# Rows of 768 bytes and products with the identity for k and q of block 0

## The chip, the core and the metric

The kernel runs on one core of a Trainium2 chip. Its engines are TensorE (PE: matmuls, and PEld: the weight loads that go with them), VectorE (DVE), ScalarE (ACT), GpSimd (POOL) and SyncE (SP), which here issues the DMAs. The metric is the device time of one execution in microseconds; smaller is better.

## The reference

The program is an attention layer followed by a feed-forward layer. For each of 4 batches and 8 heads (768 positions, 64 numbers a head):

```python
k_sum = k.reshape(B, H, nb, block, D).max(axis=3)      # 24 blocks of 32 keys
v_sum = v.reshape(B, H, nb, block, D).mean(axis=3)
scores_l = scale * q @ k^T   # only where |row - column| < 16
scores_s = scale * q @ k_sum^T + log(block)
a = softmax(concat(scores_l, scores_s))
attn = a @ concat(v, v_sum)
```

Then `x = attn` as 3072 tokens of 512 numbers, `h = x @ w_in` (512 x 2048), `g = h * cos(h)`, `out = g @ w_out` (2048 x 512). All is float32.

## The kernel before

The 3072 tokens are cut into 8 blocks of 384 (half a batch each). A block's attention is four groups of two heads, named `a`, `b`, `c`, `d`; so `a0` is group a of block 0, `d1` group d of block 1. For a group, k and q have to stand with the 64 numbers of a head on partitions and the positions along the free axis. The two heads lie on partitions 0 to 63 and 64 to 127.

The feed-forward layer runs in steps: a step takes 128 of the 2048 columns of `w_in`, multiplies them with a block's x (lines 726 and 738, 384 columns a matmul), forms the gate on ACT and DVE, and multiplies with 128 rows of `w_out` (line 786, 512 columns a matmul). Weights come in through a slice: DMA (lines 391, 395), two steps on ACT (403, 409), a join and a high part on DVE (416, 372), a low part on DVE or POOL (376).

The order of all work on all engines is written out by hand in one string, `ORDER`. Each token is a unit: `a0.tk.1.5` turns the second half of k of group a0 into bank 5, `a0.cq.v` copies the turned q out on VectorE, `a0.ks.0` takes the block maxima of k, `a0.sc` the scores, `a0.ex` the exponentials, `h7.w.5` is a matmul of the identity with itself that has no use for the result, `w1.lo.p` the low part of weight slice 1 on GpSimd. Every engine works through its instructions in this order; SP issues all DMAs of the start in one queue, and an issue that waits holds up those behind it.

In blocks 0 and 1 (where the first string of `TURNS` is 0) q is loaded as it lies in memory, 128 positions by partition in three chunks, and turned by TensorE, three transposes of 128 x 128 for each group (`turn_q`, line 503). k is loaded once for a batch, with block 0, and covers both halves: six chunks, six transposes (`turn_k`, line 516). From block 2 on VectorE does the turning. A chunk of a head is 64 float32, so a DMA packet of these loads has 256 bytes; one DMA is issued for each head (line 454). There are 16 of them for block 0, and 9216 packets: for each of four groups 2 x 128 x 6 of k and 2 x 128 x 3 of q.

Of the kernel before, what the change touches and what calls it, by code (L numbers as in the profile page):

```python
# [180 lines left out]
def tile_kernel(  # L181
# [11 lines left out]
    nc = tc.nc  # L193

    B, H, S, D = q.shape
    NT, DM = out.shape
    DF = w_in.shape[1]
    P = 128
# [6 lines left out]
    TB = S // 2  # L205
    U = TB // QT
    NG = NPAIR
    QC = TB // P
# [66 lines left out]
    ident = const.tile([P, P], F32, name="ident")  # L275
# [79 lines left out]
    def bank(i):  # L355
        return banks[:, i, :]
# [72 lines left out]
    class Group:  # L429
# [29 lines left out]
        def load_q(self):  # L459
            if self.qn is None:  # L460
                self.qn = att.tile([P, QC, P], F32, name="qn")
            self.load_heads(self.qn, q[self.b, :, self.base : self.base + TB, :], self.squares)

        def load_k(self):
            if self.kn is None:
                self.kn = att.tile([P, KC, P], F32, name="kn")
            self.load_heads(self.kn, k[self.b], self.squares)

        def load_v(self):
            b, h0, base, vn = self.b, 2 * self.pr, self.base, self.vn  # L470
# [28 lines left out]

        def turn_q(self, i):  # L500
            self.qT = bank(i)[:, :TB]
            for c in range(QC):
                nc.tensor.transpose(out=self.qT[:, c * P : (c + 1) * P], in_=self.qn[:, c, :], identity=ident)

# [6 lines left out]
                eng.tensor_scalar_mul(self.qd, self.qT, -SCALE)  # L511

        def turn_k(self, half, i):
            kT = self.kT[half] = bank(i)[:, :TB]
            for c in range(QC):
                nc.tensor.transpose(  # L516
                    out=kT[:, c * P : (c + 1) * P], in_=self.kn[:, half * QC + c, :], identity=ident
                )

        def square_q(self):  # L520
            nc.vector.transpose(out=self.qd, in_=self.qn.rearrange("p c n -> p (c n)"))
# [405 lines left out]
    class Warm:  # L927

        def products(self, i):
# [11 lines left out]
            q="load_q", k="load_k", v="load_v", m="load_vs", tq="turn_q", tk="turn_k", qt="square_q", kt="square_k", pt="square_p", po="move_out", pi="move_in", cq="place_q",  # L941
# [95 lines left out]
```

## Time and profile before

| | |
|---|---|
| median of 3 runs | 633.5 us (633.4 to 634.74) |
| the profiled execution | 633.6 us, of which its span is 631.9 us |
| PE busy | 621.1 us (98%) |
| DVE, ACT, POOL busy | 422.1, 323.9, 204.6 us |
| chain that ended last | PE 92%, DVE 4%, SP's queue 2% |

Times in the rows count from the span's start. A busy share is an average over stages: the first 62 us hold the attention of blocks 0 and 1 beside the first steps of the feed-forward layer, and the other 570 us mostly the feed-forward layer. Matmuls overlap in the array, so the distance between two starts tells more of their price than the duration of one. PE's granted clock is shown as 1.00 in all stretches.

### The profile page before, as it was taken

How to read it: one execution, taken by the hardware profiler on the slowest of the kernel's cores; microseconds unless marked ns; L12 is line 12 of the kernel's file. 1: busy time of each engine (PE TensorE's matmuls, PEld its weight loads, DVE VectorE, ACT ScalarE, POOL GpSimd, SP SyncE). 2: the span in 40 equal slices, each digit the busy share in tenths (PEclk: the TensorE clock that was granted, in tenths of full speed). 3: DMA queues.
4: the chain of work that ended last, by engine and by line, in shares of the span. 5: the costliest groups of instructions: out<-in, count | busy, mean ns of one | idle time of the engine just before them, and what ended most of it. 6: DMA issues, size and time to landing. Idle time of an engine off the chain costs nothing.

```text
span 631.9 us, 12130 instructions
## 1 busy us (share of the span) xinstructions
PE 621.1 (98%) x4568; PEld 544.3 (86%) x4568; DVE 422.1 (67%) x814; ACT 323.9 (51%) x606; POOL 204.6 (32%) x218
## 2 busy tenths in 40 slices
PE   8989999999999999999999999999999999999997
PEld 5667989889889889898988898898898988889895
DVE  4789897896666677577766765656766676544334
ACT  3888886776544454445563634344443463422222
POOL 6593422344503341234452431221431232100101
PEclk9999999999999999999999999999999999999999
DMA  9989939624455447423444544513432431400001
GB/s 223 261 220 272 297 123 250 145 54 123 122 143 133 112 95 174 102 61 108 109 110 126 117 93 102 121 47 77 108 98 61 117 75 56 114 35 17 1 1 50
DMA packets 170058, 73.52 MB, mean 116 GB/s; under 512 B 136848, under 2 KB 158864, under 8 KB 170000
## 3 DMA queue, kind: packets, MB, share of 16 engines
q1 hardware_dynamic: 169856, 72.62, 45.3%
q8 instruction: 36, 0.59, 0.4%
q14 instruction: 22, 0.18, 0.1%
q10 hardware_dynamic: 144, 0.13, 0.1%
HBM read 54.43 MB, written 16.52 MB: 112 GB/s over the span
## 4 chain that ended last, share of the span: by engine, by line
PE 92%; DVE 4%; SPq 2%; DMA 1%; issue 1%; ACT 1%; POOL 0%; POOLq 0%; DVEq 0%
PE banks L786 41%; PE banks L726 40%; PE banks L683 3%; PE banks L567 3%; PE banks L930 1%; SPq L475 1%; DVE stage L416 1%; PE banks L738 1%; PE banks L579 1%; SPq L483 1%; PE banks L516 0%; PE banks L909 0%; DMA late<-in_v_dram 0%; DMA x<-in_v_dram 0%; DVE kd L535 0%
## 5 line engine op out<-in xcount | busy, mean ns | idle before, releaser
L726 PE MATMUL banks<-xh,w 128*128 128x384 f32 x976 | 255.5, 337 | 0.5 <-DVE t L758 0.5
L786 PE MATMUL banks<-w,gh 128*128 128x512 f32 x768 | 196.5, 392 | 0.1
L726 PEld LDWEIGHTS banks<-xh,w 128*128 128x128 f32 x976 | 176.8, 188 | 3.1 <-issue 0.8
L786 PEld LDWEIGHTS banks<-w,gh 128*128 128x128 f32 x768 | 142.6, 188 | 31.4 <-DVE gh L372 1.8
L726 PE MATMUL banks<-xl,w 128*128 128x384 f32 x488 | 163.2, 334 | 0.0
L376 POOL TENSOR_TENSOR gl<-t,gh 128x384 fp32r<-128x384 f32 x63 | 65.9, 1048 | 283.3 <-DVE gh L372 147.8
L746 ACT ACTIVATE t<-banks 128x384 int32<-128x384 f32 x128 | 62.0, 488 | 126.8 <-PE banks L726 59.7
L749 DVE SCALAR_TENSOR_TENSOR t<-t,banks 128x384 f32<-128x384 int32 x128 | 69.1, 546 | 68.3 <-ACT t L746 67.6
L786 PE MATMUL banks<-w,gl 128*128 128x512 f32 x384 | 108.0, 392 | 0.0
L754 ACT ACTIVATE t<-t 128x384 f32<-128x384 f32 x128 | 65.9, 523 | 63.4 <-DVE t L749 63.1
L726 PEld LDWEIGHTS banks<-xl,w 128*128 128x128 f32 x488 | 91.6, 188 | 0.4
L758 DVE TENSOR_TENSOR t<-t,banks 128x384 f32<-128x384 f32 x128 | 69.4, 547 | 33.1 <-ACT t L754 32.1
L786 PEld LDWEIGHTS banks<-w,gl 128*128 128x128 f32 x384 | 71.6, 188 | 15.7 <-POOL gl L376 0.5
L370 ACT CAST gh<-t 128x384 fp32r<-128x384 f32 x66 | 33.5, 511 | 43.5 <-DVE t L758 25.5
L630 POOL TENSOR_TENSOR sc<-sc,r 128x720 f32<-128x720 f32 x28 | 39.0, 1392 | 43.5 <-DVE r L627 41.0
L602 POOL TENSOR_TENSOR sc<-sc,m 128x720 f32<-128x720 f32 x24 | 34.3, 1433 | 49.6 <-DVE m L594 49.6
L376 DVE TENSOR_TENSOR gl<-t,gh 128x384 fp32r<-128x384 f32 x65 | 36.8, 569 | 12.5 <-ACT gh L370 7.5
L372 DVE CAST gh<-t 128x384 fp32r<-128x384 f32 x62 | 23.1, 373 | 18.1 <-PE banks L786 14.9
L586 DVE SCALAR_TENSOR_TENSOR sc<-banks,mask 128x360 f32<-128x360 f32 x48 | 24.5, 523 | 12.5 <-PE banks L567 12.2
L620 DVE TENSOR_REDUCE r<-sc 128x6 f32<-128x726 f32 x24 | 21.6, 902 | 13.8 <-ACT sc L609 13.8
L376 POOL TENSOR_TENSOR w<-stage,w 128x1024 fp32r<-128x1024 f32 x8 | 19.8, 2470 | 31.3 <-DVE w L372 20.0
L609 ACT ACTIVATE sc<-sc 128x720 f32<-128x720 f32 x24 | 19.4, 807 | 19.0 <-POOL sc L602 18.8
(121 smaller groups left out, 621.4 us busy)
## 6 DMA issues: line engine op xcount, KB each, us to landing
pd<-stage SPq DMA_DIRECT2D x24, 384.0 KB
late<-in_moe_w_out_dram SPq DMA_DIRECT2D x16, 511.6 KB
late<-in_moe_w_in_dram SPq DMA_DIRECT2D x16, 510.5 KB
pt<-pd SPq DMA_DIRECT2D x72, 96.0 KB
vn<-in_v_dram SPq DMA_DIRECT2D x50, 120.0 KB
out_dram<-stage SPq DMA_DIRECT2D x23, 256.0 KB
kn<-in_v_dram SPq DMA_DIRECT2D x24, 192.0 KB
kn<-in_k_dram SPq DMA_DIRECT2D x48, 96.0 KB
```

The lines of the kernel that those rows point to most:

```text
L370: eng.copy(out=out, in_=in_)
L372: eng.tensor_copy(out=out, in_=in_)
L376: eng.tensor_tensor(out=lo, in0=src, in1=hi.bitcast(F32), op=ALU.subtract)
L586: nc.vector.scalar_tensor_tensor(out=self.sc.rearrange("p (c h) n -> p c h n", h=2)[:, :, hh, :], in0=self.sp[hh], scalar=SCALE, in1=mask[ ...
L602: nc.gpsimd.tensor_tensor(out=self.sc, in0=self.sc, in1=self.m.unsqueeze(2).broadcast_to([P, U, NK]), op=ALU.subtract)
L630: nc.gpsimd.tensor_tensor(out=self.sc, in0=self.sc, in1=self.r.unsqueeze(2).broadcast_to([P, U, NK]), op=ALU.mult)
L726: nc.tensor.matmul(out=self.h, lhsT=w_of(name, self.f)[:, c * P : (c + 1) * P], rhs=x_of(self.blk, part, c), start=n == 0, stop=n == last,)
L746: nc.scalar.activation(out=self.t.bitcast(I32), in_=self.h, func=AF.Copy, scale=1.0 / TWO_PI, bias=0.25)
L749: nc.vector.scalar_tensor_tensor(out=self.t, in0=self.t.bitcast(I32), scalar=-TWO_PI, in1=self.h, op0=ALU.mult, op1=ALU.add)
L754: nc.scalar.activation(out=self.t, in_=self.t, func=AF.Sin, scale=-1.0, bias=-0.5 * math.pi)
L758: nc.vector.tensor_tensor(out=self.t, in0=self.t, in1=self.h, op=ALU.mult)
L786: nc.tensor.matmul(out=accs[self.run][i], lhsT=g[:, i * P : (i + 1) * P], rhs=w_of(name, self.f), start=self.first and n == 0, stop=self.l ...
```

## The change

For block 0 alone, q and k are loaded with three neighbouring positions in one row: partition p holds positions 3p, 3p+1 and 3p+2 of a head (of k two such halves), 192 float32 or 768 bytes in one packet. That is still one DMA for each head, and 3072 packets for the 16 DMAs. Chunk c of a head then holds every third position. The turn is no longer a transpose of a chunk of both heads: it is one product with the identity for each head and chunk, with the chunk (128 partitions, 64 columns) as weights and the identity (128 columns) as the moving operand. Its 64 x 128 result goes to the partitions of its head, into every third column from c on, so that the positions stand in their order. `turn_q` of block 1 and everything behind the turns are as before; so is `ORDER`.

```diff
         def load_q(self):
             if self.qn is None:
                 self.qn = att.tile([P, QC, P], F32, name="qn")
-            self.load_heads(self.qn, q[self.b, :, self.base : self.base + TB, :], self.squares)
+            src = q[self.b, :, self.base : self.base + TB, :]
+            if self.blk:
+                self.load_heads(self.qn, src, self.squares)
+            else:
+                self.load_rows(self.qn, src)
+
+        def load_rows(self, t, src):
+
+            n = t.shape[1] // QC
+            view = t.rearrange("p c n -> p (c n)").rearrange("p (h m x) -> p h m x", h=2, m=n)
+            for hh in range(2):
+                nc.sync.dma_start(
+                    out=view[:, hh],
+                    in_=src[2 * self.pr + hh].rearrange("(m p c) d -> p m (c d)", p=P, c=QC),
+                )
+
+        def turn_rows(self, to, t, half):
+
+            n = t.shape[1] // QC
+            view = t.rearrange("p c n -> p (c n)").rearrange("p (h m c d) -> p h m c d", h=2, m=n, c=QC)
+            to = to.rearrange("p (n c) -> p n c", c=QC)
+            for c in range(QC):
+                for hh in range(2):
+                    nc.tensor.matmul(
+                        out=to[hh * D : (hh + 1) * D, :, c], lhsT=view[:, hh, half, c], rhs=ident,
+                        start=True, stop=True,
+                    )
...
         def turn_q(self, i):
             self.qT = bank(i)[:, :TB]
+            if not self.blk:
+                self.turn_rows(self.qT, self.qn, 0)
+                return
...
         def turn_k(self, half, i):
-            kT = self.kT[half] = bank(i)[:, :TB]
-            for c in range(QC):
-                nc.tensor.transpose(
-                    out=kT[:, c * P : (c + 1) * P], in_=self.kn[:, half * QC + c, :], identity=ident
-                )
+            self.kT[half] = bank(i)[:, :TB]
+            self.turn_rows(self.kT[half], self.kn, half)
```

`load_k` calls `load_rows` in the same way. On PE the first units of the program stood so before (L930 are the matmuls without use, L516 turns of k, L554 masks, L503 turns of q, L579 scores; `late_105` holds k of group a, `late_107` and `late_106` hold q of b and a):

```order
L930 MATMUL banks<-ident 128x512 x3
L516 MATMUL banks<-ident,late_105 128x128 x6
L554 LDWEIGHTS early
L554 MATMUL banks<-early 128x360
L554 LDWEIGHTS early
L554 MATMUL banks<-early 128x360
L503 MATMUL banks<-ident,late_107 128x128 x3
L503 MATMUL banks<-ident,late_106 128x128 x3
L930 MATMUL banks<-ident 128x512
L579 MATMUL banks<-kd_93,qd 64x96
```

They stand so now, the lines behind the insertion 29 further on, and both kinds of turn on line 485:

```order
L959 MATMUL banks<-ident 128x512 x3
L485 MATMUL banks<-ident,late_105 64x128 x12
L583 LDWEIGHTS early
L583 MATMUL banks<-early 128x360
L583 LDWEIGHTS early
L583 MATMUL banks<-early 128x360
L485 MATMUL banks<-ident,late_107 64x128 x6
L485 MATMUL banks<-ident,late_106 64x128 x6
L959 MATMUL banks<-ident 128x512
L608 MATMUL banks<-kd_93,qd 64x96
```

Nothing has changed its place; each turn of three products has become one of six. The other turns of block 0 on PE, behind the scores of group a, stood so before (`x_2_116` is k of c, `late_105` k of b, `late_108` q of c, `kn` k of d):

```order
L516 MATMUL banks<-ident,x_2_116 128x128 x6
L516 MATMUL banks<-ident,late_105 128x128 x3
L930 MATMUL banks<-ident 128x512
L503 MATMUL banks<-ident,late_108 128x128 x3
L930 MATMUL banks<-ident 128x512
L516 MATMUL banks<-ident,kn 128x128 x3
L516 MATMUL banks<-ident,late_105 128x128 x3
L516 MATMUL banks<-ident,kn 128x128 x3
L554 LDWEIGHTS early
```

and stand so now:

```order
L485 MATMUL banks<-ident,x_2_116 64x128 x12
L485 MATMUL banks<-ident,late_105 64x128 x6
L959 MATMUL banks<-ident 128x512
L485 MATMUL banks<-ident,late_108 64x128 x6
L959 MATMUL banks<-ident 128x512
L485 MATMUL banks<-ident,kn 64x128 x6
L485 MATMUL banks<-ident,late_105 64x128 x6
L485 MATMUL banks<-ident,kn 64x128 x6
L583 LDWEIGHTS early
```

Here too the matmuls between the turns have kept their places. The twelfth turn, q of group d, comes later, behind the turn of q of a1.

## Rows read from the trace of the kernel before

**Rows 1.** The chain that ended last, in order of time: start, length (us), what.
```profile
1.44 5.49 PE banks L930 x6
...
62.22 0.37 DVE gh L372
62.64 2.33 PE banks L786 x9
```
**Rows 2.** Busy time by stretch: length, then PE, PEld, DVE, ACT, POOL; clock, DMA share, GB/s.
```profile
0.00:20.00 20.00, 17.77 (x198) 10.95 (x199) 10.93 (x44) 9.61 (x27) 10.79 (x37) 1.00 1.07 236
23.88:42.28 18.40, 16.43 (x302) 12.05 (x302) 15.70 (x38) 13.38 (x56) 17.88 (x16) 1.00 0.81 214
44.97:62.64 17.67, 15.91 (x143) 13.26 (x142) 17.25 (x26) 15.56 (x34) 8.04 (x7) 1.00 1.05 272
62.64:600.00 537.36, 536.88 (x3660) 477.84 (x3661) 360.79 (x674) 270.24 (x450) 162.27 (x153) 1.00 0.42 107
```
**Rows 3.** Timeline, DVE, POOL, ACT: start, length, what, idle before it and its releaser.
```profile
20.50 0.56 DVE L511 TENSOR_SCALAR qd<-banks 128x384 f32<-128x384 f32 x1 [1.21 <-PE banks L503]
...
23.88 2.36 POOL L376 TENSOR_TENSOR w<-stage,w 128x1024 fp32r<-128x1024 f32 x1 [7.23 <-DVE w L372]
...
42.31 1.16 ACT L403 ACTIVATE stage<-late 128x1024 f32<-128x1024 int8 x1 [0.96 <-POOL w L376]
43.50 1.39 ACT L409 ACTIVATE first<-stage 128x1024 int8<-128x1024 f32 x1
...
44.97 2.09 DVE L416 SCALAR_TENSOR_TENSOR stage<-late,first 128x1024 int32<-128x1024 int32 x1 [0.33 <-POOL sc L630]
```
**Rows 4.** Timeline, PE up to 20 us.
```profile
6.72 1.28 PE L516 MATMUL banks<-ident,late 128*128 128x128 f32 x6
7.84 0.47 PE L554 MATMUL banks<-early 128*128 128x360 bf16 x2
8.14 0.82 PE L503 MATMUL banks<-ident,late 128*128 128x128 f32 x6
8.80 1.06 PE L930 MATMUL banks<-ident 128*128 128x512 f32 x2
...
10.80 0.87 PE L516 MATMUL banks<-ident,x 128*128 128x128 f32 x6
11.93 0.52 PE L516 MATMUL banks<-ident,late 128*128 128x128 f32 x3 [0.25 <-DMA late<-in_k_dram]
12.28 1.02 PE L930 MATMUL banks<-ident 128*128 128x512 f32 x2
13.14 0.49 PE L503 MATMUL banks<-ident,late 128*128 128x128 f32 x3
13.47 1.02 PE L930 MATMUL banks<-ident 128*128 128x512 f32 x2
14.71 0.55 PE L516 MATMUL banks<-ident,kn 128*128 128x128 f32 x3 [0.22 <-ACT sc L614]
...
19.01 1.12 PE L930 MATMUL banks<-ident 128*128 128x512 f32 x2
19.98 0.49 PE L503 MATMUL banks<-ident,late 128*128 128x128 f32 x3
```
**Rows 5.** Timeline, PE: products of 24 weight columns, by turns on two partition ranges.
```profile
23.93 2.78 PE L909 MATMUL banks<-late,early 128*24 128x256 f32 x24
26.63 0.55 PE L503 MATMUL banks<-ident,late 128*128 128x128 f32 x3
```
**Rows 6.** DMA packets from 7 to 9 us, then from 16.5 to 17.2 us.
```profile
DMA packets 1721, 0.43 MB, mean 216 GB/s; under 512 B 1721, under 2 KB 1721, under 8 KB 1721
...
DMA packets 264, 0.20 MB, mean 288 GB/s; under 512 B 2, under 2 KB 264, under 8 KB 264
```
**Rows 7.** Timeline, SP's queue: start of an issue, length, what.
```profile
19.63 1.07 SPq L246 DMA_DIRECT2D kn<-in_v_dram  x1
...
26.10 0.91 SPq L454 DMA_DIRECT2D qn<-in_q_dram  x2
```

More of the change, by code (lines that the diff above doesn't have):

```diff
@@ L466, in load_k @@
                 self.kn = att.tile([P, KC, P], F32, name="kn")
-            self.load_heads(self.kn, k[self.b], self.squares)
+            if self.squares:
+                self.load_heads(self.kn, k[self.b], True)
+            else:
+                self.load_rows(self.kn, k[self.b])
         def load_v(self):
```

## The prediction

> **What bounds the kernel now.** I read the chain that ended last first. From 62.64 us on it is TensorE to the end, released there by VectorE's copy of a gate at 62.22 [rows 1], and the stretches agree: from 62.64 to 600 us PE is busy for 536.88 of 537.36 us [rows 2]. All that this change touches lies before 21 us. So it is worth what it moves that one point at 62.64, where VectorE hands over to PE.
>
> I then went back from there through the stretches and the timelines of the engines that are full. From 44.97 to 62.64 us VectorE is full, 17.25 of 17.67 us. It begins there with the join of a weight slice (L416), behind ACT's two steps for that slice at 42.31 and 43.50, the first of which had waited for GpSimd's low part of another slice. GpSimd is full from 23.88 to 42.28, 17.88 of 18.40 us; before that it had waited 7.23 us for VectorE's high part of slice 1 [rows 2, 3]. VectorE does that behind the copy of q of a1 at 20.50, and this copy waited 1.21 us for PE (L503, the turn of q of a1) [rows 3]. The reader is to see one path: PE's turn of q of a1 at 19.98 [rows 4], VectorE, 18.4 us of GpSimd, ACT, 17.7 us of VectorE, PE. GpSimd and VectorE leave 0.52 + 0.42 = 0.94 us of slack on it. What comes late at PE's 19.98 comes late at the end.
>
> Last I read PE up to there [rows 4]. It has to wait for a load of k or q once, 0.25 us at 11.93. Its start is set by the six passes without use, 5.49 us [rows 1], not by k: the first turn follows them without a wait.
>
> **What a turn costs.** Six transposes of q stand from 8.14 to 8.80: 0.11 us each, so 0.33 for a turn. A float32 product that is no transpose is two passes (the order has one L930 where the trace has two). One pass of 512 columns takes (13.14 - 12.28) / 2 = 0.43 us, so 128 columns take 0.1075 [rows 4]. Where the weights fill only part of the array's columns, two passes run side by side: of L909, which goes by turns to two ranges of partitions, 24 passes of 256 columns stand in 26.63 - 23.93 = 2.70 us, 0.1125 each, where one alone would take 0.215 [rows 5]. The new products go by turns to partitions 0 to 63 and 64 to 127, so I take them in pairs: a turn is 3 chunks x 2 passes x 0.1075 = 0.65 us, or 0.32 more than before. Both ends: a turn cannot fall under its 0.33, since its pairs stream twice the columns; without overlap it is 12 x 0.1075 = 1.29, or 0.96 more. No row writes every third column; I take that as free by the same nearest row, and leave its risk in the upper end.
>
> A change between 128 and 64 or fewer weight columns costs something too. The same two passes of L930 take 13.14 - 12.28 = 0.86 us between transposes, and 19.98 - 19.01 = 0.97 behind scores (64 columns) [rows 4]; L909 takes 0.12 over its 24 x 0.1075 [rows 5]. So 0.1 us for each change. TensorEngine Tiling (Array Packing) of the Trainium skill, Tiling Modes, says that a change of tiling mode drains the engine, and gives no price; the two rows agree. Without that price the sum below would be 0.9 us less.
>
> **The sum, on PE up to the turn of q of a1.** Eleven of the twelve new turns lie there.
> - The first two turns begin at 6.72. The passes before run at 5.49 / 6 = 0.92 us, half the later rate, so the clock is at its 1.2 GHz level although it is shown as granted in full; of the first six transposes, 7.84 - 6.72 = 1.12 us instead of 0.66, about the first 0.94 us still go at that rate. The new turns begin 0.1 us later: two chunk steps at 0.43 and four at 0.215 make 1.72, 0.60 more; with a change of columns ahead and one behind, 0.80.
> - Two turns of q: 2 x 0.32 + 0.2 = 0.84. The pass at 8.80 and the scores of a behind it are late by 1.64.
> - Two turns of k of c, one of b: 0.96, and 0.1 on leaving (the change into them is there today). PE idles about 0.4 us today between 10.80 + 0.66 and 11.93; k of b will have landed, so this goes. Late by 2.30.
> - q of c: 0.32 + 0.2. Late by 2.82.
> - Then three turns, behind a wait of 14.71 - 13.47 - 0.86 = 0.38 us for ACT's exponentials of a. These are released by the scores and by the first turn of c, so they move by 1.64 + 0.32 = 2.0 only; what is late next is PE itself: 2.82 + 0.1 - 0.38 = 2.54. The three turns add 0.96 and 0.1: 3.6.
>
> From there ACT's copy, VectorE's maxima and the scores of b, which wait for the last of them, lead to PE's 19.01 and 19.98 [rows 4]; I round to 3.5 us for the turn of q of a1. GpSimd's low part of slice 1 then begins at about 27.4 instead of 23.88, and nothing on the path gives it back but the 0.94 us of slack, which I leave in the range. The twelfth turn, 0.32 + 0.1, lies beside GpSimd's work.
>
> **The loads.** The 9216 packets of 256 bytes are 2.36 MB, and move at 216 GB/s; packets of 768 bytes (of v) move at 288 GB/s [rows 6]. That is 10.9 us against 8.2, 2.7 less. I cost this gain at nothing beyond the 0.4 us above: PE waits for nothing else of these loads. The number of issues on SP is the same, and none is moved. SP's issue of v at 19.63 and of q of d1 at 26.10 [rows 7] wait for turns that get longer (k of d, then about 19.2; q of d0, then about 24.5), but end no later than they are issued today. The queue behind is ahead, until it waits for VectorE's and GpSimd's sums, which are late with the rest.
>
> So the profiled execution, 633.6 us, becomes 633.6 + 3.5 = **637.1 us**; it is 0.1 us over the median of the runs, so I give the same number for that. With the ends of this case, no price for a change of columns and all slack given back, 633.6 + 3.5 - 0.9 - 0.9 = 635.3; above, up to 638.5, if PE's 0.4 us for the twelfth turn and 1 us of other delays reach the path.
>
> **Rivals.**
> - *The late head is absorbed.* PE is idle for 18.40 - 16.43 = 1.97 and 17.67 - 15.91 = 1.76 us in the two stretches [rows 2], together 3.73, enough for 3.5. Then 633.6. Against it: that is not where the path runs; GpSimd and VectorE have 0.94.
> - *No overlap, or slow writes into every third column.* 0.64 more for each of eleven turns, 7 us, and 0.3 in the slow part at the start: 644.4. For it: no row has 64 weight columns with 128 moving ones, nor a write with a stride. Against it: L909, whose pairs overlap fully.
> - *Faster: the loads bound the head.* The DMA share is over 1 in the first 20 us [rows 2], and all loads share one queue. If GpSimd's start hung on a landing, the 2.7 us would reach the end, and longer turns would hide in today's waits: 633.6 - 2.7 = 630.9. It decides once the landing of weight slice 1 or of v is later than PE's turns; today slice 1 is joined by VectorE behind a wait for PE. DMA: Bandwidth & Descriptors of the Trainium skill, Specifications, names 512 bytes as the least for line rate, which speaks for this; rows 6 agree in direction.
>
> **How the numbers follow.** The forecast 0.72; absorbed 0.11; no overlap 0.10; faster 0.07. A measurement of this kernel cannot tell 0.2%, or 1.3 us, from no change. Slower is then 0.72 + 0.10 = 0.82, the same 0.11, faster 0.07. The range of the forecast alone is 635.3 to 638.5; to leave out no more than 2 in 10 it goes down to 633.4, taking in the absorbed case, and up to 640.5, for turns between paired and single passes.
>
> **What would show it.** The products of a turn in pairs, a turn at 0.65 us; the pass at 8.80 at about 10.4, the one at 19.01 at 22.5; VectorE's copy of q of a1 at 24.0 behind a wait for PE; GpSimd's low part of slice 1 at 27.4, ACT's step of 42.31 at about 45.8, PE's first product behind the handover at 66.1, and from there the same length to the end. I am wrong if PE waits for DMA where it now waits for ACT, if GpSimd has gaps between 27 and 46 us that let it catch up, or if the 3.5 us at 20 us are no longer there at 62.

## The result: 638.15 us, 0.63% slower

The changed kernel takes 638.15 us in the median of 5 runs (637.29 to 639.17). The kernel before took 633.5 us beside it (633.4 to 635.55). The ratio is 1.0063 [1.0048, 1.0078]. The profiled execution took 637.89 us with a span of 636.2, against 633.6 and 631.9 before: 4.3 us more. A second set of runs of the same changed kernel (e9 below) gave 637.04 and 1.0052 [1.0038, 1.0066]. The forecast was 637.1 us.

Lines behind the new functions stand 29 further down in the changed kernel: L786 is now L815, L930 is L959, L554 is L583, L503 is L535. L485 is the new product of a turn.

The timeline of PE in the changed kernel, up to the turn of q of a1 (start and length in us, what, idle before it and its releaser), which answers to [rows 4]:

```profile
1.44 4.95 PE L959 MATMUL banks<-ident 128*128 128x512 f32 x6 [1.44 <-POOL ident masks.py:199]
6.32 1.53 PE L485 MATMUL banks<-ident,late 128*64 128x128 f32 x24
7.78 0.48 PE L583 MATMUL banks<-early 128*128 128x360 bf16 x2
8.19 1.53 PE L485 MATMUL banks<-ident,late 128*64 128x128 f32 x24
9.65 1.12 PE L959 MATMUL banks<-ident 128*128 128x512 f32 x2
...
11.72 1.53 PE L485 MATMUL banks<-ident,x 128*64 128x128 f32 x24
13.09 0.82 PE L485 MATMUL banks<-ident,late 128*64 128x128 f32 x12
13.84 1.13 PE L959 MATMUL banks<-ident 128*128 128x512 f32 x2
...
15.70 1.12 PE L959 MATMUL banks<-ident 128*128 128x512 f32 x2
16.76 0.88 PE L485 MATMUL banks<-ident,kn 128*64 128x128 f32 x12
17.46 0.82 PE L485 MATMUL banks<-ident,late 128*64 128x128 f32 x12
18.12 0.82 PE L485 MATMUL banks<-ident,kn 128*64 128x128 f32 x12
18.88 0.78 PE L583 MATMUL banks<-early 128*128 128x360 bf16 x4
...
23.02 0.49 PE L535 MATMUL banks<-ident,late 128*128 128x128 f32 x3
```

A turn is now 12 instructions (two passes for each of six products) and takes 18.12 - 17.46 = 0.66 us between starts, where a transposed one took 0.33. Two turns with the change of columns behind them take 9.65 - 8.19 = 1.46 us, against 0.66; the change ahead shows in the masks before them, 8.19 - 7.78 = 0.41 us instead of 0.30. Up to 18.88 no row has a wait: those for k of b (11.93) and for ACT (14.71) of [rows 4] are gone, and PE runs through. The turn of q of a1 begins at 23.02, 3.04 us late.

The path behind it, in the same timeline on DVE, POOL and ACT, answers to [rows 3], its last line to [rows 1]:

```profile
23.54 0.56 DVE L543 TENSOR_SCALAR qd<-banks 128x384 f32<-128x384 f32 x1 [1.21 <-PE banks L535]
...
26.91 2.36 POOL L376 TENSOR_TENSOR w<-stage,w 128x1024 fp32r<-128x1024 f32 x1 [9.00 <-DVE w L372]
...
45.35 1.16 ACT L403 ACTIVATE stage<-late 128x1024 f32<-128x1024 int8 x1 [0.95 <-POOL w L376]
...
48.01 2.09 DVE L416 SCALAR_TENSOR_TENSOR stage<-late,first 128x1024 int32<-128x1024 int32 x1 [0.33 <-POOL sc L659]
...
65.27 0.36 DVE L372 CAST gh<-t 128x384 fp32r<-128x384 f32 x1
```

Against 20.50, 23.88, 42.31, 44.97 and 62.22 these are 3.04, 3.03, 3.04, 3.04 and 3.05 us late. The delay is passed from engine to engine without loss or gain. The busy times of the last three stretches, moved by the delay (length, then PE, PEld, DVE, ACT, POOL; clock, DMA share, GB/s), answer to [rows 2]:

```profile
26.91:45.35 18.44, 16.66 (x314) 12.39 (x307) 15.93 (x38) 13.70 (x58) 17.89 (x16) 1.00 0.62 169
48.01:65.69 17.68, 15.47 (x142) 13.25 (x142) 16.82 (x26) 15.14 (x34) 8.04 (x7) 1.00 1.00 240
65.69:600.00 534.31, 533.21 (x3640) 473.76 (x3640) 362.90 (x674) 270.68 (x450) 161.36 (x153) 1.00 0.42 109
```

The two stretches are as long as before (18.44 against 18.40, 17.68 against 17.67), and PE's idle time in them, 1.78 and 2.21 us, gave nothing back. In the last stretch PE is idle for 1.10 us where it was idle for 0.48: something is lost there. It is at 122 us, in this execution of the changed kernel:

```profile
121.63 2.40 POOL L376 TENSOR_TENSOR w<-stage,w 128x1024 fp32r<-128x1024 f32 x1 [9.61 <-DVE w L372]
...
121.66 2.79 DVE L376 TENSOR_TENSOR gl<-t,gh 128x384 fp32r<-128x384 f32 x1
```

and in the kernel before, which had the two the other way round:

```profile
118.97 0.55 DVE L376 TENSOR_TENSOR gl<-t,gh 128x384 fp32r<-128x384 f32 x1
...
119.13 2.66 POOL L376 TENSOR_TENSOR w<-stage,w 128x1024 fp32r<-128x1024 f32 x1 [9.75 <-DVE w L372]
```

GpSimd began 0.03 us ahead of VectorE, and VectorE's subtraction then took 2.79 us instead of 0.55. PE's delay goes from 3.0 us there to 4.0 at 126.03 (before: 121.99), and stays at about 4.3 to the end. So 3.05 us of the profiled 4.3 come from the turns, and 1.25 from this meeting.

Of the loads, the stretch from 7 to 9 us answers to [rows 6], now with packets of 768 bytes for most:

```profile
DMA packets 846, 0.61 MB, mean 306 GB/s; under 512 B 50, under 2 KB 846, under 8 KB 846
```

306 GB/s instead of 216. No row above starts earlier for it. The wait of 0.25 us for k of b is gone, but not by the loads: e2 below, with the loads of before, comes to that row at 13.24 and does not wait either.

### The profile page after: what moved, and what is told of

It reads as the page before. It is cut to its first block, busy times and chain, and to the rows that moved or that the text cites. A ratio compares the mean times of both kernels' runs of the same rounds, so it can differ in the third digit from the quotient of the medians.

```text
span 636.2 us, 12341 instructions
## 1 busy us (share of the span) xinstructions
PE 625.1 (98%) x4676; PEld 547.1 (86%) x4676; DVE 424.0 (67%) x814; ACT 324.2 (51%) x606; POOL 204.3 (32%) x218
## 4 chain that ended last, share of the span: by engine, by line
PE 94%; DVE 2%; DMA 2%; ACT 1%; SPq 1%; issue 0%; POOL 0%; POOLq 0%; DVEq 0%
PE banks L815 41%; PE banks L755 40%; PE banks L712 4%; PE banks L596 3%; PE banks L959 2%; PE banks L485 1%; PE banks L767 1%; DMA late<-in_v_dram 1%; PE banks L608 1%; PE banks L668 0%; PE banks L938 0%; DVE first L372 0%; DMA pt<-pd 0%; DVE stage L682 0%; DVE stage L416 0%
## 5 line engine op out<-in xcount | busy, mean ns | idle before, releaser
L815 PE MATMUL banks<-w,gh 128*128 128x512 f32 x768 | 196.7, 392 | 0.6 <-ACT gh L370 0.6
L815 PEld LDWEIGHTS banks<-w,gh 128*128 128x128 f32 x768 | 142.5, 188 | 32.2 <-DVE gh L372 1.8
L815 PE MATMUL banks<-w,gl 128*128 128x512 f32 x384 | 108.1, 392 | 0.0
L787 DVE TENSOR_TENSOR t<-t,banks 128x384 f32<-128x384 f32 x128 | 69.4, 547 | 33.1 <-ACT t L783 32.0
L815 PEld LDWEIGHTS banks<-w,gl 128*128 128x128 f32 x384 | 71.5, 188 | 16.2 <-POOL gl L376 0.5
L376 DVE TENSOR_TENSOR gl<-t,gh 128x384 fp32r<-128x384 f32 x65 | 39.0, 603 | 12.6 <-ACT gh L370 7.5
```

Of the source, the lines that this page charges most:

```text
L376: eng.tensor_tensor(out=lo, in0=src, in1=hi.bitcast(F32), op=ALU.subtract)
L787: nc.vector.tensor_tensor(out=self.t, in0=self.t, in1=self.h, op=ALU.mult)
L815: nc.tensor.matmul(out=accs[self.run][i], lhsT=g[:, i * P : (i + 1) * P], rhs=w_of(name, self.f), start=self.first and n == 0, stop=self.l ...
```

## The experiments

Medians of the kernel before in the three sets were 633.89 (e1 to e4), 633.76 (e5 to e8) and 633.78 (e9 to e12); each set ran on a chip of its own. The diffs of `ORDER` below show the changed ends of its long lines only.

**e1_rows_only: the new loads with the old transposes.** On the changed kernel:

```diff
         def turn_rows(self, to, t, half):
-            n = t.shape[1] // QC
-            view = t.rearrange("p c n -> p (c n)").rearrange("p (h m c d) -> p h m c d", h=2, m=n, c=QC)
-            to = to.rearrange("p (n c) -> p n c", c=QC)
             for c in range(QC):
-                for hh in range(2):
-                    nc.tensor.matmul(
...
+                nc.tensor.transpose(out=to[:, c * P : (c + 1) * P], in_=t[:, half * QC + c, :], identity=ident)
```

> The loads of the change alone: rows of 768 bytes, but three transposes of 128 neighbouring columns for a turn, as many as before. The columns that a transpose takes are then not the ones that belong together, so the result is not the reference's; the work on every engine is that of before. Theory 1 (the turns on TensorE make the change slow, the loads only take away one wait of 0.4 us): 632.8 to 633.6 us, the turn of q of a1 at 19.6 to 20.0. Rival (the loads themselves matter, for example through the queue behind them): over 635 us if they are what costs, or under 631.5 if their 2.7 us reach the end.

633.76 us (633.53 to 635.83), ratio 0.9999 [0.9990, 1.0007]. PE in e1:

```profile
11.36 0.49 PE L481 MATMUL banks<-ident,late 128*128 128x128 f32 x3
11.68 1.02 PE L952 MATMUL banks<-ident 128*128 128x512 f32 x2
...
14.55 0.55 PE L481 MATMUL banks<-ident,kn 128*128 128x128 f32 x3 [0.66 <-ACT sc L636]
...
19.81 0.49 PE L528 MATMUL banks<-ident,late 128*128 128x128 f32 x3
```

The wait for k of b is gone, and the passes of 12.28 begin 0.60 us earlier. Three rows on, the wait for ACT's exponentials is 0.66 us instead of 0.22, and of the 0.60 only 0.16 is left at the turn of q of a1. Not even that is the loads': e4 below, with the loads of before, has that turn at 19.82; both came out of the start 0.12 us sooner than the profile of before (first masks at 7.72 and 7.71 instead of 7.84). The loads are worth nothing that these runs can tell.

**e2_products_only: the old loads, turned by products.** On the kernel before:

```diff
+        def turn_heads(self, to, t, half):
+            for c in range(QC):
+                for hh in range(2):
+                    nc.tensor.matmul(
+                        out=to[hh * D : (hh + 1) * D, c * P : (c + 1) * P],
+                        lhsT=t[:, half * QC + c, hh * D : (hh + 1) * D], rhs=ident, start=True, stop=True,
+                    )
```

It takes the place of the transposes of block 0.

> The turns of the change alone: loads in packets of 256 bytes as before, each turn six products of 64 weight columns with the identity, written to neighbouring columns. Theory 1: the turn of q of a1 is late by 3 to 3.9 us (it keeps the wait for k of b), the point where TensorE takes over at 62.6 by the same, so 636.5 to 637.4 us, and 1.2 us more if GpSimd again begins the low part of slice 11 just ahead of VectorE. Rival (loads cost): under 635 us.

637.41 us (636.68 to 638.45), ratio 1.0050 [1.0036, 1.0063]. PE in e2:

```profile
8.34 1.53 PE L511 MATMUL banks<-ident,late 128*64 128x128 f32 x24
9.80 1.13 PE L938 MATMUL banks<-ident 128*128 128x512 f32 x2
```

Two turns take 1.46 us, as in the changed kernel, though these products write a whole range of columns and not every third one. So the strided write costs nothing, and the products with the old loads lose as much as the whole change does, as far as the scatter between its two sets (637.04 and 638.15) lets one tell. Its profiled execution ends 4.4 us late, 3.19 of them at the turn of q of a1 (23.17), and VectorE and GpSimd don't meet in it: VectorE's subtraction takes 0.55 us at 123.87.

**e3_changed_s11_behind and e4_before_s11_behind: VectorE's subtraction kept ahead of GpSimd's low part.** In `ORDER` the high part of slice 11, which releases GpSimd's low part, goes behind the subtraction `s12.lo.0.v`; e3 is the changed kernel with this, e4 the kernel before:

```diff
-s14.dl w11.hi.v
-s13.si s12.lo.0.v c2.kt.0
+s14.dl
+s13.si s12.lo.0.v w11.hi.v c2.kt.0
```

> The changed kernel, with one token of the order moved: VectorE's high part of weight slice 11 behind the low part of step 12, so that GpSimd cannot begin its low part of that slice ahead of VectorE's. Theory 2 (1.25 of the 4.3 us come from one collision at 121.6 us, where VectorE's subtraction took 2.79 instead of 0.55 us because GpSimd had begun 0.03 us before it): the subtraction takes about 0.55 us, the shift stays at 3.05 us to the end, 636.6 to 637.2 us. Rival (the second loss has another cause, for example TensorE waits there for something else that is late): 638.15 us as the changed kernel.

> The kernel before with the same token moved, as a control of the experiment on the changed kernel. Theory 2: nothing to win, since the collision is not there: 633.3 to 633.9 us. Rival (the move is worth 1.25 us by itself): 632.3 us.

e3: 637.06 us (636.70 to 638.28), 1.0049 [1.0037, 1.0061]; its subtraction takes 0.56 us, and its delay is 3.0 us at the gate and 3.25 at the end. e4: 633.96 (633.45 to 636.46), 1.0003 [0.9994, 1.0013]. That looked like 1.1 us won in e3, until the changed kernel and e3 were both run once more (below).

**e5_heads_apart: the products of one head, then those of the other.** On the changed kernel:

```diff
-            for c in range(QC):
-                for hh in range(2):
+            for hh in range(2):
+                for c in range(QC):
```

> The changed kernel with the two loops of a turn exchanged: three products of one head, then three of the other, the same 64 x 128 products. Theory 1 (a turn costs 0.66 us because two passes on different column ranges run side by side): products of one head can't run beside each other, a turn takes 1.1 to 1.3 us, eleven turns on the path give 5 to 7 us more than the changed kernel, 643 to 645 us. Rival (a turn is bound by something else, for example its weight loads or the issue of twelve passes): about 638 us.

638.17 us (637.69 to 638.47), 1.0065 [1.0052, 1.0078]: not the 643 that a loss of the overlap would have given. PE in e5:

```profile
8.62 1.80 PE L485 MATMUL banks<-ident,late 128*64 128x128 f32 x24
10.35 1.12 PE L959 MATMUL banks<-ident 128*128 128x512 f32 x2
...
13.78 0.27 PE L485 MATMUL banks<-ident,late 128*64 128x128 f32 x1
13.84 0.27 PE L485 MATMUL banks<-ident,x 128*64 128x128 f32 x1
13.89 0.27 PE L485 MATMUL banks<-ident,late 128*64 128x128 f32 x1
13.95 0.27 PE L485 MATMUL banks<-ident,x 128*64 128x128 f32 x1
```

Two turns take 1.73 us, 0.27 more than when the heads alternate. The last rows show why it isn't more: products of the next turn (`late`, k of b) go by turns with those still left of the turn before (`x`, k of c), 0.05 us apart. PE started these on the free half of the array though they were issued behind others for the busy half. My idea that the overlap needs heads in turn falls. This run's head is later by 1.5 us than the changed kernel's (VectorE's gate at 66.74 instead of 65.27) and its median is the same; in its profile VectorE and GpSimd don't meet, and the 4.5 us of the gate are 4.6 at the end.

**e6_before_no_h6, e7_changed_no_h, e8_before_w1_first: PE passes without use on the path.** If the path runs through PE up to the turn of q of a1, taking other work off PE there must show. e6 is the kernel before without the pair h6 (L930 at 19.01); e7 is e3 without h6, h5 and h1; e8 is e6 with the high part of slice 1 ahead of the copy of q of a1:

```diff
-h6.w.2 a1.tq.6 a1.ms.1.4 v0_1.l
+a1.tq.6 a1.ms.1.4 v0_1.l
```

```diff
-a0.mx.0 w1.l.6 h5.w.1
-a1.q c0.tq.0 h1.w.1 d0.q
...
-h6.w.2 a1.tq.6
+a0.mx.0 w1.l.6
+a1.q c0.tq.0 d0.q
...
+a1.tq.6
```

```diff
-d0.tq.2 a1.cq.v
...
-c1.q w1.fb a0.nm
-w1.hi.v a0.tp.1.3
+d0.tq.2 w1.fb w1.hi.v a1.cq.v
...
+c1.q a0.nm
+a0.tp.1.3
```

> The kernel before without one of its matmuls that have no use for the result, h6, the two passes at 19.01 us just ahead of the turn of q of a1. Theory 3 (one path from PE's turn of q of a1 over VectorE, GpSimd, ACT and VectorE to PE at 62.6 us sets the end): the turn comes 1.0 us earlier, GpSimd's low part of slice 1 begins at about 22.9, and the end comes 0.7 to 1.0 us earlier: 632.7 to 633.1 us against 633.7. Rival (the first 60 us take up such shifts): no change within 0.2 us.

> The changed kernel with slice 11 as in the experiment before, and without three of the matmuls that have no use for the result (h5, h1, h6), whose place on TensorE the longer turns take. Theory 3: h5 and h1 give 0.9 us together until ACT's exponentials of a are what the turns wait for, h6 gives 1.0: 1.9 us less than 637.06, 635.0 to 635.4 us, still slower than before. Rival (the clock falls without them, or the first 60 us take it up): 637 us or more.

> The kernel before without h6 and with VectorE's join and high part of weight slice 1 ahead of its copy of q of a1, in the 1.2 us in which it waited for TensorE. Theory 3: GpSimd begins the low part of slice 1 at about 21.2 instead of 23.88, but the copy of q of a1 and all maxima behind it come 0.7 us later than without h6, so what GpSimd needs next may be what it waits for: 632.0 to 633.2 us. Rival (the path does not begin at slice 1): slower than without h6 by up to 1 us.

e6: 632.96 us (632.53 to 635.36), 0.9992 [0.9983, 1.0001]. Its turn of q of a1 begins at 18.86, 1.12 us earlier (0.95 earlier than in e1, at 19.81, so 0.17 is the start and the rest h6), GpSimd's low part of slice 1 at 22.82, 1.06 earlier, and VectorE's gate at 61.20, 1.02 earlier:

```profile
18.86 0.55 PE L503 MATMUL banks<-ident,late 128*128 128x128 f32 x3
...
22.82 2.35 POOL L376 TENSOR_TENSOR w<-stage,w 128x1024 fp32r<-128x1024 f32 x1 [6.32 <-DVE w L372]
...
61.20 0.36 DVE L372 CAST gh<-t 128x384 fp32r<-128x384 f32 x1
```

This is the path of the prediction pushed the other way, over 40 us and four engines, and it holds in this execution. Of the 1.02, the span shows 0.7; the interval of the ratio still takes in 1, and e11 below repeats it.

e7: 636.12 us (635.03 to 637.79), 1.0037 [1.0024, 1.0049]. I had expected about 1.9 us less than e3; the median is 0.94 less, and in the profiles the turn of q of a1 comes 22.94 - 21.59 = 1.35 us earlier and the end 0.8. PE in e7:

```profile
16.29 0.88 PE L485 MATMUL banks<-ident,kn 128*64 128x128 f32 x12 [1.25 <-ACT sc L643]
...
21.59 0.55 PE L535 MATMUL banks<-ident,late 128*128 128x128 f32 x3
```

Without h5 and h1 PE comes to the turns of d earlier and waits 1.25 us for ACT's exponentials, a wait that the changed kernel had filled.

e8: 633.65 us (633.03 to 636.28), 1.000 [0.999, 1.001]. GpSimd's low part of slice 1 begins at 21.18, 1.64 us earlier than in e6, and the end is no earlier. The busy times in e8:

```profile
20.00:22.00 2.00, 0.43 (x21) 0.38 (x22) 1.97 (x5) 1.49 (x8) 0.82 (x1) 1.00 1.11 324
38.00:42.00 4.00, 3.40 (x77) 2.92 (x76) 3.16 (x10) 2.29 (x13) 3.78 (x5) 0.73 0.97 245
```

PE, waiting for the copy of q of a1 that now stands behind slice 1, is busy for 0.43 of 2 us. GpSimd's next piece shows where the gain went:

```profile
25.59 1.39 POOL L630 TENSOR_TENSOR late<-late,r 128x720 f32<-128x720 f32 x1 [2.05 <-DVE r L627]
```

It waits 2.05 us for a result that VectorE gives behind the copy, and begins 0.47 us behind that of e6 (25.12). So slice 1 is not the whole of the path: the copy of q of a1, and what hangs on it, belongs to it as well. PE's granted clock, 0.73 from 38 to 42 us, is lower only after this loss; what it added this run doesn't tell.

**e9_changed_again, e10_s11_behind_again, e11_before_no_h6_again, e12_before_no_h.** The first three are the changed kernel, e3 and e6 as they were; e12 takes h7, h5, h1, h6 and h3 out of the kernel before:

```diff
-a0.ck.1.a a0.ck.0.a h7.w.5 b0.cq.a
+a0.ck.1.a a0.ck.0.a b0.cq.a
...
-v1_0.s.0.v a1.ex.0 h3.w.5
+v1_0.s.0.v a1.ex.0
```

(h5, h1 and h6 as in e7.)

> The changed kernel once more, on the same chip as the three that follow, so that they can be compared. Theory 2: the collision at 121.6 us is there in the profile again unless TensorE reaches that point in another phase; 637.5 to 638.5 us.

> The changed kernel with VectorE's high part of slice 11 behind the low part of step 12, once more. Theory 2: 0.8 to 1.3 us below the changed kernel of the same call. Rival (the two medians differed by chance): within 0.4 us of it.

> The kernel before without h6, once more. Theory 3: 0.6 to 1.0 us below the kernel before. Rival: within 0.3 us of it.

> The kernel before without five matmuls that have no use for the result (h7, h5, h1, h6, h3); the first three stay. Theory 3: h7 gives 0.2 us, h5 and h1 nothing (the turns behind them wait for ACT), h6 about 0.8, h3 nothing (GpSimd is the bound there): 632.4 to 633.0 us. Rival (the idle time that they leave lets the clock fall, as in the kernel with slice 1 ahead, where it was granted at 0.73 from 38 to 42 us): 634 us or more.

e9: 637.04 us (636.74 to 637.88), 1.0052 [1.0038, 1.0066]. At 122 us VectorE is ahead again, and its subtraction takes 0.55:

```profile
122.12 0.55 DVE L376 TENSOR_TENSOR gl<-t,gh 128x384 fp32r<-128x384 f32 x1
...
122.28 2.66 POOL L376 TENSOR_TENSOR w<-stage,w 128x1024 fp32r<-128x1024 f32 x1 [9.98 <-DVE w L372]
```

The same program meets at this place in one execution and not in another. e10: 637.54 us (636.79 to 639.22), 1.0061 [1.0048, 1.0073]; its subtraction is ahead by its order, its delay is 3.5 us at 126 us and yet 4.2 at 168. So e3's gain isn't confirmed: e3 and e10 together don't differ from the changed kernel's two sets. The meeting explains 1.25 us of one profiled execution, not the medians.

What e10 lost there its rows show:

```profile
117.89 1.13 ACT L403 ACTIVATE stage<-late 128x1024 f32<-128x1024 int8 x1 [1.83 <-DMA late<-in_moe_w_out_dram]
...
125.51 3.12 PE L815 MATMUL banks<-w,gh 128*128 128x512 f32 x12 [0.39 <-ACT gh L370]
```

This is ACT's first step for weight slice 11, and it waits 1.83 us for the slice's transfer. VectorE's join of the slice, which stands ahead of the subtraction, comes late with it, and PE waits for the gate: the delay, 3.0 us until then, is 3.8 behind it, and a wait of 0.37 for another DMA at 172.36 makes it 4.2. In the changed kernel the same step has no wait (116.01), and it is then that GpSimd comes ahead of VectorE; in e9 it waits 0.46 us, in e3 1.09, in e2 1.88. So in these profiles the loss goes with one landing: the meeting where it is early, 0.7 to 0.8 us where ACT waits 1.8 for it, and 0.1 at most in between. Why it lands at different times no run shows.

e11: 632.82 us (632.43 to 633.69), 0.9984 [0.9975, 0.9993], the fastest kernel of this study: the kernel before without h6, about 0.9 us under it, at the edge of what can be told. Its profile is 1.06 us early up to ACT's step of 42.31, but only 0.59 at VectorE's gate (61.63), since a slice landed late here too; e6 had this step at 46.42 without a wait:

```profile
47.92 1.15 ACT L403 ACTIVATE stage<-late 128x1024 f32<-128x1024 int8 x1 [1.40 <-DMA late<-in_moe_w_out_dram]
```

e12: 633.43 (632.49 to 634.88), 0.9995 [0.9986, 1.0004]. From 14 to 20 us, e12:

```profile
14.00:20.00 6.00, 5.48 (x111) 4.53 (x112) 4.11 (x10) 4.07 (x10) 1.39 (x1) 0.72 1.13 299
```

and e11:

```profile
14.00:20.00 6.00, 5.67 (x119) 4.20 (x117) 4.75 (x12) 5.04 (x16) 1.39 (x1) 1.00 1.11 295
```

Without all five, PE's granted clock is 0.72 there, behind a stretch from 8 to 14 us in which PE was busy for 3.79 of 6 us (5.32 in e11), and what the shorter work saves is lost again: its turn of q of a1 begins at 19.80. Without h6 alone the clock stays at 1.00.

## Why the prediction held, and which terms were off

The mechanism held at each station. In us late against the kernel before, the changed profile beside the prediction:

| station on PE | predicted | measured |
|---|---|---|
| first masks, behind two turns of k | 0.80 | -0.06 (7.78 to 7.84) |
| passes behind two turns of q | 1.64 | 0.85 (9.65 to 8.80) |
| passes behind k of c and b | 2.30 | 1.56 (13.84 to 12.28) |
| passes behind q of c | 2.82 | 2.23 (15.70 to 13.47) |
| first of the three turns | 2.54 | 2.05 (16.76 to 14.71) |
| turn of q of a1 | 3.5 | 3.04 (23.02 to 19.98) |
| first product behind the handover | 3.5 | 3.05 (65.69 to 62.64) |

- *A turn.* 0.65 us was worked out from L909's pairs; it is 0.66. Two turns of q with two changes of columns were to cost 0.84 more, and cost 0.85 + 0.06 = 0.91. The 0.1 us for a change came from two unlike rows and is a little low: 0.91 - 2 x 0.33 makes 0.12 each, and q of c, 0.67 - 0.33, makes 0.17 each.
- *The first term failed.* The first two turns were to cost 0.80 and cost nothing here. I had taken the masks' products at 7.84 to stand behind the turns alone, because their row shows no wait. They also need GpSimd's masks, and these end at 3.96 + 3.71 = 7.67 in the kernel before:

```profile
3.96 3.71 POOL L317 TENSOR_SCALAR_AFFINE_SELECT early<-early 128x384 bf16<-128x384 bf16 x10 [0.16 <-DVE early L326]
```

In e4, whose start is that of the kernel before, the six passes of that execution took 5.00 us instead of 5.49, and PE has to wait:

```profile
6.27 0.82 PE L516 MATMUL banks<-ident,late 128*128 128x128 f32 x6
7.71 0.47 PE L554 MATMUL banks<-early 128*128 128x360 bf16 x2 [0.62 <-POOL early L317]
```

So 0.62 us of longer turns would be covered by GpSimd there. In e10, whose passes took 4.26 us, even the longer turns of the change are covered:

```profile
7.72 0.47 PE L583 MATMUL banks<-early 128*128 128x360 bf16 x2 [0.56 <-POOL early L317]
```

The other half of the miss is the rate of those passes: I took 5.49 us as a property of the program, and it is one of the execution. In 14 profiles with the same start the six passes took from 4.26 (e10) to 5.49 us, all with a granted clock shown as 1.00. The changed kernel's first masks came at 7.78 (4.95 us), in e9 at 8.04 (5.22 us) and in e3 at 7.72 (4.77 us). The true term is thus 0 to some 0.3 us. The size of the head depends on these starts: in the five kept profiles with the change's turns (changed kernel, e2, e3, e9, e10) the turn of q of a1 begins at 22.93 to 23.28, in the three with the old turns and h6 up to there (before, e1, e4) at 19.81 to 19.98, so it is 2.95 to 3.47 us late, and the 3.5 lie just above that.
- *The rest of the head* was meant to add 2.7 behind the first term, and added 3.1: 0.91 + 0.71 + 0.67 - 0.18 + 1.08 (the masks behind the three turns, at 18.88 instead of 15.75), then back by 0.09 to 3.04. Of this, q of c (0.67 instead of 0.52) was most off.
- *The loads at nothing*: e1 shows it (ratio 0.9999). The wait for k of b went because PE came later.
- *Nothing given back between 23 and 62 us*: in the profile of the changed kernel the delay is 3.03 to 3.05 throughout, and e6 shows the same path carrying an advance. It is not so in every execution: e11 lost 0.47 us of its advance there to a late weight slice.
- *Not foreseen:* the last 1.25 us of the profiled execution, at 122 us, far behind the point where I let the argument end. That the total came out so near 637.1 is in part luck: the head was 0.45 us too large, and losses behind 62 us that I had not foreseen took its place. In the five kept profiles with the change's turns the turn of q of a1 is 2.95 to 3.3 us later than in the profile of before and the end 3.3 to 4.4; only the former is the mechanism that I forecast. In e9, whose set has the median 637.04, 3.3 us are the head and 0.2 come behind it.

Of the rivals, *absorbed* fell by the stretches (PE's idle time is there and gives nothing), *no overlap, or slow writes* by the 0.66 us of a turn and by e2, whose turns take the same without the strided write, and *the loads bound the head* by e1. What stays open is why two sets of the same changed kernel differ by 1.1 us in their medians. The landing of slice 11 makes a difference of that size between profiled executions, by the meeting in one and by the late join in e10; that the medians differ for it is not shown, and the sets may have run on different chips, or simply scatter (their intervals overlap).

## What to carry to other kernels

Follow the delay by its stations: PE, copy, slice, gate. What an edit adds on an engine that a path runs through can be followed over 40 us and four engines to the hundredth, and arrives at the end 600 us later; but on the way other transfers land early or late and add up to 1.25 us, so a profile of one execution tells the size of the edit only up to there. What an edit saves on a transfer that nobody waits for arrives as nothing, whatever the DMA share says. Where a row shows no wait, ask which other inputs it has and when they were ready: that is the cover which makes the first part of an edit free. Price a product from pairs that already run beside each other on parts of the array, and count two passes for a float32 product that is no transpose.

## What the runs showed of the hardware that was not expected

- A GpSimd operation on two tensors in SBUF and a VectorE one of the same kind don't run side by side at 122 us: the one that starts first runs at its own pace, and the other is late by the rest. VectorE's 0.55 us became 2.79 behind GpSimd's 2.40; in the other order GpSimd took 2.66 instead of 2.40. The Trainium skill (SBUF — State Buffer, section SBUF: two separate sides) says that the two engines share a pair of ports that is locked for a whole instruction, by VectorE where both its inputs lie in SBUF; both orders here agree. So does e10, where VectorE's product with a bank (L787) takes 0.52 us at 124.34 beside GpSimd's 2.39 from 124.01.
- Products for one half of the array begin ahead of products for the other half that were issued before them (13.78 ahead of 13.84 in e5): only 0.27 us are lost on two turns.
- The first six passes of PE take 4.26 to 5.49 us in executions that begin alike.
- Passes without use between 8.8 and 14.5 us keep PE's granted clock at 1.00: without h7, h5 and h1 (and h6 and h3 behind them) it is 0.72 from 14 to 20 us (e12), without h6 alone 1.00 (e11). In the changed kernel without h5, h1 and h6 (e7), where longer turns fill PE, it is 1.00 too.
